# First expert steps: sums of weight blocks on VectorE instead of GpSimd, and most of the gate inside the attention

## The chip, the cores and the metric

The kernel runs on one core of a Trainium2 chip. The metric is the device time of one execution in microseconds (us): before the change the median of 3 runs is 2134.11 us (2133.75 to 2134.13). One further execution was recorded by the profiler and gives all the rows below.

The core has five engines with their own in-order instruction queues: TensorE (PE; its weight loads are shown as PEld), VectorE (DVE), ScalarE (ACT), GpSimd (POOL) and SyncE (SP, which issues the loads here). They run side by side and wait for each other by semaphores.

## The reference

Attention over 4 batches, 8 heads, 1152 keys and 576 queries (each the mean of two neighbours), head dimension 64, and then a mixture of 8 experts on the 2304 tokens that come out:

```python
q_pool = q.reshape(B, H, S // 2, 2, D).mean(axis=3)
scores = scale * np.matmul(q_pool, k.transpose(0, 1, 3, 2))
attn = softmax(scores)                       # with + 1e-09 in the sum
x = matmul(attn, v) as (2304, 512)
logits = x @ w_gate                          # (2304, 8)
P = np.exp(logits - logits.max())
for _ in range(8):                           # Sinkhorn
    P /= P.sum(1, keepdims=True) + 1e-09
    P /= P.sum(0, keepdims=True) + 1e-09
    P *= N / E
for e in range(E):
    out += P[:, e:e+1] * (np.maximum(x @ w1[e], 0.0) @ w2[e])
```

All is float32; w1 is (8, 512, 1024), w2 (8, 1024, 512).

## The kernel before, in words

Two stages follow each other: `attention` and then `moe`.

**Attention.** There are 16 pairs (batch and two heads), each of four full query tiles and one mixed tile. Every operation is entered into a `Plan` with an engine, a cost, a priority (T, in planned microseconds; `PAIR` is the planned length of one pair) and the data and buffers that it reads and writes. `Plan.order` simulates the engines by these costs and writes out one fixed order for all queues; the buffers of a kind ("tr" is a PSUM kind with three buffers, used by transposes and the like) are handed out in order of priority. The result x lies transposed in SBUF: 512 features on partitions in four chunks, 2304 tokens along the free axis. One batch is 576 tokens, or 4.5 token tiles of 128. Near the end the plan also prepares the first token group for the experts (`Blocks`) and loads the first weight blocks and makes their sums on GpSimd (`load_first`, `sums_first`).

**Experts.** `moe` has no order written by hand: the Tile framework's scheduler orders each engine's queue. It first cuts the first w1 block into a high and a low part (`cut1`: L135 on ScalarE, L140 on VectorE), then computes the gate: for all 18 token tiles four matmuls with x as weights and 8 columns of `w_gate` as the moving side, into one PSUM tile `psl` (L630), copied to `PR` by L632. `sinkhorn` is a generator: pieces of its work (small VectorE operations L636 to L658, and an all-reduce over the partitions on GpSimd, L639 once and L654 eight times) are put between the other work by `next(fill)`, four pieces per step.

There are 96 steps: three token groups of 768 tokens, 8 experts, 4 slices of the hidden dimension. A step computes its first product by a Strassen-like scheme of 7 block products (`product`, L671 to L673, each 6 matmuls of 384 columns, since every operand is in two parts). For that, each step's w1 block needs four sums and differences of its quarters: `Weights.sums1`, L121 to L124, four tensor_tensor operations of 128x256 on GpSimd. `sums1(k + 1)` stands in step k behind the third product; `cut1(k + 1)` follows behind the fourth and needs the sums; then the load of the next but one block is issued (one buffer, w1s). VectorE adds up the products out of PSUM (L691) and, with ScalarE, cuts the hidden values (`hidden`, L680 and L681). After every second step, six second products (`second`, L708, 12 matmuls of 512 columns each) are queued, and up to three of them are issued in each of the steps that follow; their results are added to the output, which overwrites x: for the first expert without a weight (L712, L714), later weighted with PR (L717, L718).

Of the kernel before, what the change touches and what calls it, by code (L numbers as in the profile page):

```python
# [5 lines left out]
F32 = mybir.dt.float32  # L6
F32R = mybir.dt.float32r
ACTF = mybir.ActivationFunctionType
# [3 lines left out]
P = 128  # L12
# [4 lines left out]
N, D, E, F = B * Q, H * HD, 8, 1024  # L17
ND = D // P
NT = N // P
# [3 lines left out]
MT = TG // P  # L23
FQ = F // 2 // P
NPAIR = H // 2
NPAIRS = B * NPAIR
# [4 lines left out]
def attention_moe(tc, q, k, v, w_gate, w1, w2, out):  # L31

    nc = tc.nc
    with (  # L40
        tc.tile_pool(name="const", bufs=1) as const,
        tc.tile_pool(name="stage", bufs=1, reuse_waits="tile") as stage,
    ):
        ident = const.tile([P, P], F32, name="ident")
        x = const.tile([P, G, ND, TG], F32, name="x")
        wg = const.tile([P, ND, E], F32, name="wg")

        xch = const.tile([P, 7, 2, TH], F32R, name="xch")
        xcl = const.tile([P, 7, 2, TH], F32R, name="xcl")
        wt = Weights(nc, stage, w1, w2)  # L50
        blocks = Blocks(nc, stage, x, xch, xcl)

        attention(tc, q, k, v, w_gate, x, ident, wg, blocks, wt)
        moe(tc, out, x, xch, xcl, ident, wg, blocks, wt)


class Blocks:
# [32 lines left out]
class Weights:  # L90
# [24 lines left out]
    def sums1(self, k):  # L115

        r = self.raw1[k]
        a11, a12, a21, a22 = r[:, 0, 0:2], r[:, 0, 2:4], r[:, 1, 0:2], r[:, 1, 2:4]
        s = self.sums[k] = self.stage.tile([P, 4, 2, P], F32, name="w1t", tag="w1t")
        e = self.nc.gpsimd  # L120
        e.tensor_tensor(out=s[:, 0], in0=a21, in1=a22, op=ALU.add)  # L121
        e.tensor_tensor(out=s[:, 1], in0=s[:, 0], in1=a11, op=ALU.subtract)
        e.tensor_tensor(out=s[:, 2], in0=a11, in1=a21, op=ALU.subtract)
        e.tensor_tensor(out=s[:, 3], in0=a12, in1=s[:, 1], op=ALU.subtract)  # L124
# [30 lines left out]
class Plan:  # L155
# [18 lines left out]
    def op(self, eng, cost, prio, fn, r=(), w=(), new=(), use=(), lat=0, mode="", after=0):  # L174

        i = len(self.ops)
        deps = set()
        for x in r:
            deps.update(self.writers.get(x, ()))
        for x in w:  # L180
            deps.update(self.writers.get(x, ()))
            deps.update(self.readers.get(x, ()))
        for x in r:
            self.readers.setdefault(x, []).append(i)
        for x in w:
            self.writers[x] = [i]
            self.readers[x] = []
        for name, tag in new:
            self.buf[name] = tag
            self.users[name] = 0  # L190
        mine = [n for n, _ in new] + list(use)
        for n in mine:
            self.users[n] += 1
        deps.discard(i)
        self.ops.append(dict(eng=eng, cost=cost, prio=prio, fn=fn, deps=deps, new=new, mine=mine, lat=lat, mode=mode,
                             after=after, i=i))
# [102 lines left out]
PAIR = QT * UNIT + MIXED  # L299
# [7 lines left out]
    return (n * 2.1 + 150) if two else (n * 3.45 + 100)  # L307


def attention(tc, q, k, v, w_gate, xx, ident, wg, blocks, wt, dry=False, NP=NPAIRS):  # L310


    pairs = [(b, hp) for b in range(B) for hp in range(NPAIR)]
# [7 lines left out]
    D = {}  # L321
    if not dry:
        nc = tc.nc
# [21 lines left out]
    def op(eng, cost, prio, r=(), w=(), new=(), use=(), lat=0, mode="", after=0):  # L345
        def put(fn):
            plan.op(eng, cost, prio, fn, r, w, new, use, lat, mode, after)
        return put

    def pair_ops(p):  # L350
        b, hp = pairs[p]
        first = p == 0
        T = PAIR * (p - 1) if p else -60.0

        @op("SP", 1800, T - 16, w=[("raw", p)], new=[(("kr", p), "kr"), (("qr", p), "qr")], lat=2500)
        def load():
            kr = D["kr", p] = sbt([P, NC, 2, HD], F32, "kr")
            qr = D["qr", p] = sbt([P, 2 * QT + 1, 2, HD], F32, "qr")
            for h in range(2):
                x = q[b, 2 * hp + h]  # L360
                nc.sync.dma_start(out=qr[:, h * QT:(h + 1) * QT],
                                  in_=x[:2 * QM].rearrange("(t p r) d -> p t r d", p=P, r=2))
                nc.sync.dma_start(out=qr[64 * h:64 * h + 64, 2 * QT],
                                  in_=x[2 * QM:].rearrange("(p r) d -> p r d", r=2))
            for h in range(2):
                nc.sync.dma_start(out=kr[:, :, h], in_=k[b, 2 * hp + h].rearrange("(p c) d -> p c d", c=NC))

        @op("SP", 600, T - 6, w=[("v", p)], new=[(("v", p), "vt")], lat=4000)
        def load_v():
            vt = D["v", p] = sbt([P, 2, NC, HD], F32, "vt")  # L370
            nc.sync.dma_start(out=vt, in_=v[b, 2 * hp:2 * hp + 2].rearrange("h (p c) d -> p h c d", c=NC))

        ae = "DVE" if first else "Pool"

        @op(ae, cost(ae, 512, two=True) + 2 * cost(ae, 64, two=True), T + 2, r=[("raw", p)], w=[("qa", p)],
            new=[(("qa", p), "qa")], use=[("qr", p)])
# [12 lines left out]
        for i, (what, c0, n) in enumerate(groups):  # L389
            Ti = T + 6 + 3.4 * i  # L390
            src = [("qa", p)] if what == "q" else [("raw", p)]
            buf = ("qa", p) if what == "q" else ("kr", p)
            tag = what + "T"

# [174 lines left out]


    if NP == NPAIRS:
        T = PAIR * (NP - 5)
        src = [("x", p, mixed) for p in range(2 * NPAIR) for mixed in (False, True)]
        for n, i in enumerate((0, 1, 2, 3, 4, 6, 5)):
            Ti = T + PAIR * n / 3
            if i > 2:
                @op("Pool", 1800, Ti, w=[("T", i)],
                    r=src + {3: [], 4: [("T", 3)], 6: [("T", 4), ("xc", 3, 1)], 5: [("xc", 4, 1), ("T", 6)]}[i])
                def t_add(i=i):
                    blocks.add(0, i, nc.gpsimd)  # L580

            @op("ACT", cost("ACT", 2 * TH), Ti + 2.5, r=src if i < 3 else [("T", i)], w=[("xc", i, 0)])
            def xc_hi(i=i):
                blocks.hi(0, i)

            @op("DVE", cost("DVE", 2 * TH, two=True), Ti + 4, r=[("xc", i, 0)] + [("T", i)] * (i > 2), w=[("xc", i, 1)])
            def xc_lo(i=i):
                blocks.lo(0, i)

        T = PAIR * (NP - 2)  # L590

        @op("SP", 1200, T, w=[("w", 0)], lat=2500)
        def load_first():
            wt.load1(0)
            wt.load2(0)

        @op("Pool", 3000, T + 4, r=[("w", 0)], w=[("w", 1)])
        def sums_first():
            wt.sums1(0)
# [7 lines left out]
        pool.release()  # L607


def moe(tc, out, x, xch, xcl, ident, wg, blocks, wt):  # L610
    nc = tc.nc
    with (
        tc.tile_pool(name="wts", bufs=2, reuse_waits="tile") as wts,
        tc.tile_pool(name="hid", bufs=4, reuse_waits="tile") as hid,
        tc.tile_pool(name="tmp", bufs=1, reuse_waits="tile") as tmp,
        tc.tile_pool(name="gc", bufs=1, reuse_waits="tile") as gc,
        tc.tile_pool(name="gs", bufs=2, reuse_waits="tile") as gs,
        tc.tile_pool(name="ps1", bufs=4, space=PSUM, reuse_waits="tile") as ps1,
        tc.tile_pool(name="ps2", bufs=4, space=PSUM, reuse_waits="tile") as ps2,
# [3 lines left out]
        wt.load1(1)  # L623


        psl = ps2.tile([P, NT, E], F32, name="psl", tag="ps2")
        for m in range(NT):
            g, i = divmod(m, MT)
            for c in range(ND):
                nc.tensor.matmul(psl[:, m, :], x[:, g, c, i * P:(i + 1) * P], wg[:, c, :], start=(c == 0), stop=(c == ND - 1))  # L630
        PR = gc.tile([P, NT, E], F32, name="PR")
        nc.scalar.activation(out=PR, in_=psl, func=ACTF.Copy)  # L632

        def sinkhorn():
            mx = gs.tile([P, 1], F32, name="gmx", tag="gmx")
            nc.vector.tensor_reduce(out=mx, in_=PR, axis=AX.XY, op=ALU.max)  # L636
            yield
# [3 lines left out]
            nc.vector.tensor_scalar(out=nm, in0=mxa, scalar1=-1.0, scalar2=None, op0=ALU.mult)  # L641
            nc.scalar.activation(out=PR, in_=PR, func=ACTF.Exp, bias=nm)
            yield
            for _ in range(8):
                rs = gs.tile([P, NT], F32, name="rs", tag="rs")
                nc.vector.tensor_reduce(out=rs, in_=PR, axis=AX.X, op=ALU.add)
                nc.vector.tensor_scalar(out=rs, in0=rs, scalar1=1e-9, scalar2=None, op0=ALU.add)
                nc.vector.reciprocal(rs, rs)
                nc.vector.tensor_tensor(out=PR, in0=PR, in1=rs.unsqueeze(2).to_broadcast([P, NT, E]), op=ALU.mult)
                cs = gs.tile([P, E], F32, name="cs", tag="cs")  # L650
                nc.vector.tensor_reduce(out=cs, in_=PR.rearrange("p n e -> p e n"), axis=AX.X, op=ALU.add)
                yield
# [77 lines left out]
        for k in range(wt.steps):  # L730
            g, r = divmod(k, FQ * E)
# [60 lines left out]
```

## Time and profile before

| what | value |
|---|---|
| median of 3 runs | 2134.11 us |
| the profiled execution, by its own time | 2129.85 us |
| its span, first to last instruction | 2127.7 us |
| mean granted TensorE clock | 0.984 of full |
| TensorE busy (matmul) | 2073.7 us, 97% |
| VectorE busy | 1468.2 us, 69% |
| ScalarE busy | 900.2 us, 42% |
| GpSimd busy | 363.2 us, 17% |
| attention | 0 to about 538.8 us |
| gate | 538.8 to 565.8 us |
| expert steps | 565.8 us to the end |

Busy times are shares of one execution; an engine that is not the bottleneck may be idle at no cost. Matmuls overlap each other, so that a busy TensorE is not TensorE at its peak, and a matmul's own duration is longer than its distance to the next one. A float32 matmul of the gate appears as two records (144 records of L630 for 72 matmuls). "Issue" in a list of waits is time in which an engine waited for nothing that the profile shows. A granted clock of 1.00 is 2.4 GHz, 0.50 is 1.2 GHz.

### The profile page before, as it was taken

The numbers are of one execution on the slowest core, as the hardware profiler recorded it, in microseconds if no ns is written. First come the engines' busy times: TensorE is split into PE (matmuls) and PEld (weight loads), VectorE is DVE, ScalarE is ACT, GpSimd is POOL, SyncE is SP. The second block draws the span as 40 slices with busy tenths as digits, with TensorE's granted clock in tenths as the row PEclk, the third lists the DMA queues.
The fourth block names the chain that finished last, engine by engine and source line by source line (L and its number), as shares of the span: only waits on it lengthen the run. The fifth ranks groups of instructions, "written<-read, shape, count | busy, mean of one in ns | idle before, by whom it ended". The sixth has DMA issues, their size and how long they took to land.

```text
span 2127.7 us, 34487 instructions
## 1 busy us (share of the span) xinstructions
PE 2073.7 (97%) x13664; PEld 1832.1 (86%) x13664; DVE 1468.2 (69%) x3024; ACT 900.2 (42%) x1594; POOL 363.2 (17%) x456
## 2 busy tenths in 40 slices
PE   9999999999975899999999999999999999999999
PEld 7888888888965899998989999899999999989988
DVE  6666677666344777777776777777778677777774
ACT  5766777666321333333334333333343433333331
POOL 1000101100011322121232211212112221121210
PEclk9999999999788999999999999999999999999999
DMA  5111221200110222221213222222123122222211
GB/s 154 46 57 46 57 68 46 57 24 13 40 60 30 60 78 61 77 62 60 80 55 95 79 70 61 69 70 69 60 79 99 52 78 70 63 67 71 69 60 40
DMA packets 191953, 135.93 MB, mean 64 GB/s; under 512 B 44080, under 2 KB 160816, under 8 KB 191792
## 3 DMA queue, kind: packets, MB, share of 16 engines
q1 hardware_dynamic: 191792, 133.74, 20.9%
q8 instruction: 107, 1.75, 0.3%
q14 instruction: 54, 0.44, 0.1%
HBM read 128.99 MB, written 4.72 MB: 63 GB/s over the span
## 4 chain that ended last, share of the span: by engine, by line
PE 93%; issue 2%; DVE 2%; POOL 1%; DMA 1%; ACT 1%; SPq 0%; POOLq 0%; DVEq 0%; ACTq 0%
PE pso L708 35%; PE psh L671 11%; PE psh L673 11%; PE psh L672 11%; PE tr L488 8%; PE S L448 7%; PE av L516 7%; PE tr L406 1%; PE psl L630 1%; PE tr L545 1%; DVE c L691 0%; DMA w2s<-in_moe_w_dram 0%; DVE hl L681 0%; DVE xcl L87 0%; ACT w1h L135 0%
## 5 line engine op out<-in xcount | busy, mean ns | idle before, releaser
L671 PE MATMUL psh<-xch,w1h 128*128 128x384 f32 x1344 | 457.3, 340 | 44.0 <-ACT w1h L135 41.4
L680 ACT ACTIVATE hh<-c 128x384 fp32r<-128x384 f32 x384 | 200.0, 521 | 674.8 <-DVE c L691 674.8
L673 PE MATMUL psh<-xch,w1l 128*128 128x384 f32 x1344 | 455.2, 340 | 0.0
L672 PE MATMUL psh<-xcl,w1h 128*128 128x384 f32 x1344 | 454.7, 338 | 0.0
L708 PE MATMUL pso<-w2h,hl 128*128 128x512 f32 x1152 | 453.5, 394 | 0.8 <-DVE hl L681 0.8
L708 PE MATMUL pso<-w2l,hh 128*128 128x512 f32 x1152 | 452.9, 393 | 0.0
L708 PE MATMUL pso<-w2h,hh 128*128 128x512 f32 x1152 | 448.0, 389 | 0.0
L718 DVE SCALAR_TENSOR_TENSOR x<-pso,PR,x 128x512 f32<-128x512 f32 x264 | 197.4, 749 | 179.8 <-PE pso L708 179.7
L671 PEld LDWEIGHTS psh<-xch,w1h 128*128 128x128 f32 x1344 | 255.6, 190 | 57.7 <-ACT w1h L135 43.9
L455 DVE TENSOR_SCALAR_CACHE_REDUCE E<-S 128x384 f32<-128x384 f32 x432 | 227.0, 554 | 53.9 <-PE S L448 53.7
L672 PEld LDWEIGHTS psh<-xcl,w1h 128*128 128x128 f32 x1344 | 255.5, 190 | 10.1
L121 POOL TENSOR_TENSOR w1t<-w1s 128x256 f32<-128x256 f32 x96 | 75.2, 784 | 1089.3 <-DMA w1s<-in_moe_w_dram 959.7
L708 PEld LDWEIGHTS pso<-w2h,hl 128*128 128x128 f32 x1152 | 216.0, 188 | 47.0 <-DVE hl L681 1.3
L673 PEld LDWEIGHTS psh<-xch,w1l 128*128 128x128 f32 x1344 | 254.8, 190 | 1.4 <-DVE w1l L140 1.3
L708 PEld LDWEIGHTS pso<-w2l,hh 128*128 128x128 f32 x1152 | 216.1, 188 | 40.2
L708 PEld LDWEIGHTS pso<-w2h,hh 128*128 128x128 f32 x1152 | 216.5, 188 | 39.3 <-ACT hh L680 0.3
L681 DVE SCALAR_TENSOR_TENSOR hl<-c,hh 128x384 fp32r<-128x384 f32 x384 | 240.3, 627 | 13.4 <-ACT hh L680 1.4
L498 ACT ACTIVATE ET<-tr 128x512 f32<-128x512 f32 (+2 forms) x288 | 142.5, 531 | 116.7 <-PE tr L488 116.7
L691 DVE TENSOR_TENSOR c<-psh,u 128x384 f32<-128x384 f32 x288 | 150.9, 553 | 57.3 <-PE psh L673 55.8
L448 PE MATMUL S<-kT,qT 64*128 64x384 f32 (+1 forms) x1296 | 183.2, 365 | 1.7 <-DVE E L455 1.4
L488 PE MATMUL tr<-ident,E 128*128 128x128 f32 x1296 | 182.9, 279 | 0.3 <-DVE ET L500 0.3
L471 ACT ACTIVATE E<-E,st 128x1152 f32<-128x1152 f32 x144 | 179.8, 1253 | 6.0 <-DVE st L461 4.0
(77 smaller groups left out, 2250.9 us busy)
## 6 DMA issues: line engine op xcount, KB each, us to landing
w1s<-in_moe_w_dram SPq DMA_DIRECT2D x192, 256.0 KB, 3.0
w2s<-in_moe_w_dram SPq DMA_DIRECT2D x96, 512.0 KB, 3.5
kr<-in_k_dram SPq DMA_DIRECT2D x32, 288.0 KB, 3.9
vt<-in_v_dram SPq DMA_DIRECT2D x16, 576.0 KB, 3.8
qr<-in_q_dram SPq DMA_DIRECT2D x32, 256.0 KB, 4.1
out_dram<-x SPq DMA_DIRECT2D x18, 256.0 KB, 2.2
qr<-in_q_dram SPq DMA_DIRECT2D x32, 32.0 KB, 3.8
wg<-in_moe_w_gate_dram SPq DMA_DIRECT2D x1, 16.0 KB, 4.8
```

Of the source, the lines that this page charges most:

```text
L448: nc.tensor.matmul(ps[:, h, :PK], D["qT", p][rows, x, t * P:(t + 1) * P], D["kT", p][rows, y, j * PK:(j + 1) * PK], start=(i == 0), stop=( ...
L455: nc.vector.tensor_scalar(out=D["E", m][:, h, j * PK:(j + 1) * PK], in0=D["sc", m, j][:, h, :PK], scalar1=1.0, scalar2=None, op0=ALU.mult, ...
L471: nc.scalar.activation(out=x, in_=x, func=ACTF.Exp, bias=D["st", m][:, h, 3:4], accum_out=D["rs", p][:, t, h:h + 1])
L488: nc.tensor.transpose(ps[:, i * P:(i + 1) * P], x[:, c * P:(c + 1) * P], ident)
L671: nc.tensor.matmul(ps, hi[:, a, c, :], xch[:, b, c, :], start=(c == 0), stop=False)
L672: nc.tensor.matmul(ps, hi[:, a, c, :], xcl[:, b, c, :], start=False, stop=False)
L673: nc.tensor.matmul(ps, lo[:, a, c, :], xch[:, b, c, :], start=False, stop=(c == 1))
L680: nc.scalar.activation(out=hh[:, fh, ts], in_=src, func=ACTF.Relu)
L681: nc.vector.scalar_tensor_tensor(out=hl[:, fh, ts], in0=src, scalar=0.0, in1=hh[:, fh, ts].bitcast(F32), op0=ALU.max, op1=ALU.subtract)
L691: nc.vector.tensor_tensor(out=y, in0=ps, in1=t, op=ALU.add)
L708: nc.tensor.matmul(ps, u[:, fh, ms], w[:, fh, :], start=(n == 0), stop=(n == 11))
L718: nc.vector.scalar_tensor_tensor(out=a, in0=ps, scalar=PR[:, m, e:e + 1], in1=a, op0=ALU.mult, op1=ALU.add)
```

## The change

Two edits. In `Weights.sums1`, the four operations of the blocks 1 to 8 (`2 * FQ` is 8) are issued on VectorE; block 0 and blocks 9 and up stay on GpSimd. And the gate of the token tiles 0 to 12 is computed within the attention's plan: tiles 0 to 8 (tokens of batches 0 and 1) from one pair behind batch 1, tiles 9 to 12 (with batch 2) from one pair behind batch 2, each three planned microseconds behind the one before, each in a "tr" buffer, and copied to PR by VectorE. `moe` computes the last five tiles only. PR moves into the pool of constants.

```diff
+        PR = const.tile([P, NT, E], F32, name="PR")
...
+def gate(nc, ps, x, wg, m):
+
+    g, i = divmod(m, MT)
+    for c in range(ND):
+        nc.tensor.matmul(ps, x[:, g, c, i * P:(i + 1) * P], wg[:, c, :], start=(c == 0), stop=(c == ND - 1))
...
-        e = self.nc.gpsimd
+        e = self.nc.vector if 0 < k <= 2 * FQ else self.nc.gpsimd
...
     if NP == NPAIRS:
+        for bs, lo_m, hi_m in (((0, 1), 0, 9), ((2,), 9, 13)):
+            for m in range(lo_m, hi_m):
+                T = PAIR * (NPAIR * (bs[-1] + 1) + 1) + 3 * (m - lo_m)
+
+                @op("PE", 4 * 115, T, mode="F", r=[("wg",)] + [("x", p, mixed) for p in range(NPAIR * (bs[-1] + 1)) for mixed in (False, True)],
+                    w=[("gt", m)], new=[(("gt", m), "tr")])
+                def gate_mm(m=m):
+                    D["gt", m] = pst([P, 512], "tr")
+                    gate(nc, D["gt", m][:, :E], xx, wg, m)
+
+                @op("DVE", 90, T + 0.5, r=[("gt", m)], w=[("PR", m)], use=[("gt", m)])
+                def gate_out(m=m):
+                    nc.vector.tensor_copy(PR[:, m], D["gt", m][:, :E])
...
-        psl = ps2.tile([P, NT, E], F32, name="psl", tag="ps2")
-        for m in range(NT):
-            g, i = divmod(m, MT)
-            for c in range(ND):
-                nc.tensor.matmul(psl[:, m, :], x[:, g, c, i * P:(i + 1) * P], wg[:, c, :], start=(c == 0), stop=(c == ND - 1))
-        PR = gc.tile([P, NT, E], F32, name="PR")
-        nc.scalar.activation(out=PR, in_=psl, func=ACTF.Copy)
+        M0 = 13
+        psl = ps2.tile([P, NT - M0, E], F32, name="psl", tag="ps2")
+        for m in range(M0, NT):
+            gate(nc, psl[:, m - M0], x, wg, m)
+        nc.scalar.activation(out=PR[:, M0:], in_=psl, func=ACTF.Copy)
```

## Rows read from the trace of the kernel before

**Rows 1.** Page, part 2: busy tenths and granted clock in 40 slices.
```profile
PE   9999999999975899999999999999999999999999
...
PEclk9999999999788999999999999999999999999999
```
**Rows 2.** Windows; columns: window, length, PE, PEld, DVE, ACT, POOL busy, PEclk, DMA.
```profile
300.00:530.00 230.00, 230.00 (x2631) 191.70 (x2628) 156.90 (x531) 162.30 (x304) 15.43 (x16) 1.00 0.14 39
794.00:1100.00 306.00, 306.00 (x1527) 275.96 (x1526) 225.85 (x354) 104.13 (x178) 64.40 (x80) 1.00 0.23 69
```
**Rows 3.** Windows: the gate at either clock, and the expert steps 0 to 7.
```profile
538.77:542.80 4.03, 4.03 (x40) 4.03 (x37) 2.48 (x4) 3.05 (x5) 0.00 (x0) 1.00 0.19 55
542.80:565.80 23.00, 23.00 (x110) 23.00 (x110) 0.00 (x0) 0.00 (x0) 0.00 (x0) 0.50 0.05 15
565.80:730.00 164.20, 120.56 (x555) 107.43 (x556) 96.36 (x207) 46.35 (x77) 30.83 (x41) 0.86 0.17 52
```
**Rows 4.** Waits, 565.8 to 730 us: us in total, times, longest.
```profile
PE psh L671 <- ACT w1h L135: 41.4, 6, 14.5
...
ACT w1h L135 <- POOL w1t L124: 50.1, 8, 17.3
```
**Rows 5.** Timeline of POOL: start us, us, line, operation [idle before <-releaser].
```profile
621.95 0.43 POOL L654 PARTITION_ALL_REDUCE ca<-cs  x1 [5.80 <-issue]
629.41 0.71 POOL L122 TENSOR_TENSOR w1t<-w1t,w1s 128x256 f32<-128x256 f32 x1 [7.03 <-issue]
```
**Rows 6.** Waits of POOL, 565.8 to 730 us.
```profile
POOL w1t L122 <- issue: 30.0, 4, 8.0
...
POOL w1t L121 <- DMA w1s<-in_moe_w_dram: 11.4, 3, 4.0
```
**Rows 7.** Windows: the four stretches of the expert steps at the lower clock.
```profile
565.80:570.10 4.30, 4.30 (x14) 4.30 (x15) 1.44 (x3) 1.60 (x4) 1.15 (x1) 0.50 0.25 62
632.60:638.40 5.80, 5.77 (x17) 5.33 (x18) 3.28 (x5) 1.04 (x2) 0.33 (x1) 0.50 0.30 90
664.00:669.20 5.20, 5.20 (x15) 4.76 (x16) 3.26 (x5) 1.05 (x2) 0.00 (x0) 0.50 0.34 100
694.20:700.00 5.80, 5.76 (x17) 5.32 (x18) 3.37 (x5) 1.04 (x2) 0.43 (x1) 0.51 0.30 90
```
**Rows 8.** Timeline of PE: first and last products of a run at either clock.
```profile
566.27 0.52 PE L672 MATMUL psh<-xcl,w1h 128*128 128x384 f32 x1
...
569.79 0.52 PE L671 MATMUL psh<-xch,w1h 128*128 128x384 f32 x1
...
571.03 0.34 PE L671 MATMUL psh<-xch,w1h 128*128 128x384 f32 x1
...
577.11 0.33 PE L673 MATMUL psh<-xch,w1l 128*128 128x384 f32 x1
```
**Rows 9.** Timeline of DVE around the start of the gate.
```profile
539.15 0.23 DVE L558 TENSOR_TENSOR x<-tr,avs 128x64 f32<-128x64 f32 x1 [1.69 <-ACT avs L535]
...
541.13 1.23 DVE L140 TENSOR_TENSOR w1l<-w1t,w1h 128x1024 fp32r<-128x1024 f32 x1 [0.23 <-ACT w1h L135]
```
**Rows 10.** Timeline of PE at the end of the attention.
```profile
527.79 1.48 PE L516 MATMUL av<-ET,vt 128*64 128x128 f32 x24
...
536.91 0.33 PE L488 MATMUL tr<-ident,E 128*128 128x128 f32 x1 [0.35 <-DVE ET L500]
```
**Rows 11.** Groups by line and shape, 565 to 730 us: busy us, mean ns, idle before.
```profile
L140 DVE TENSOR_TENSOR w1l<-w1t,w1h 128x1024 fp32r<-128x1024 f32 x8 | 9.8, 1224 | 30.3 <-ACT w1h L135 30.3
...
L140 DVE TENSOR_TENSOR w1l<-w1s,w1h 128x256 fp32r<-128x256 f32 x8 | 3.4, 426 | 0.4 <-ACT w1h L135 0.4
...
L123 POOL TENSOR_TENSOR w1t<-w1s 128x256 f32<-128x256 f32 x8 | 7.0, 874 | 0.0
```
**Rows 12.** Windows late in the expert steps 0 to 7.
```profile
711.00:730.00 19.00, 16.30 (x86) 15.11 (x87) 14.99 (x24) 7.11 (x13) 7.31 (x8) 1.00 0.30 84
...
720.00:725.00 5.00, 4.15 (x24) 4.12 (x24) 5.00 (x8) 2.26 (x5) 3.40 (x4) 1.00 0.14 39
```
**Rows 13.** Window with short stops, and the longest stop in it on PE's timeline.
```profile
577.30:602.00 24.70, 20.68 (x100) 17.70 (x98) 15.37 (x35) 10.70 (x17) 6.08 (x8) 1.00 0.27 84
...
602.08 0.44 PE L671 MATMUL psh<-xch,w1h 128*128 128x384 f32 x1 [2.16 <-ACT w1h L135]
```

More of the change, by code (lines that the diff above doesn't have):

```diff
@@ L51, in attention_moe @@
         blocks = Blocks(nc, stage, x, xch, xcl)
-        attention(tc, q, k, v, w_gate, x, ident, wg, blocks, wt)
-        moe(tc, out, x, xch, xcl, ident, wg, blocks, wt)
+        attention(tc, q, k, v, w_gate, x, ident, wg, PR, blocks, wt)
+        moe(tc, out, x, xch, xcl, wg, PR, blocks, wt)
+def gate(nc, ps, x, wg, m):
+    g, i = divmod(m, MT)
+    for c in range(ND):
+        nc.tensor.matmul(ps, x[:, g, c, i * P:(i + 1) * P], wg[:, c, :], start=(c == 0), stop=(c == ND - 1))
 class Blocks:
@@ L307, in cost, with attention @@
     return (n * 2.1 + 150) if two else (n * 3.45 + 100)
-def attention(tc, q, k, v, w_gate, xx, ident, wg, blocks, wt, dry=False, NP=NPAIRS):
+def attention(tc, q, k, v, w_gate, xx, ident, wg, PR, blocks, wt, dry=False, NP=NPAIRS):
     pairs = [(b, hp) for b in range(B) for hp in range(NPAIR)]
@@ L571, in attention @@
     if NP == NPAIRS:
+        for bs, lo_m, hi_m in (((0, 1), 0, 9), ((2,), 9, 13)):
[9 more added lines that the diff above has]
+                    nc.vector.tensor_copy(PR[:, m], D["gt", m][:, :E])
+    if NP == NPAIRS:
         T = PAIR * (NP - 5)
@@ L607, in attention, with moe @@
         pool.release()
-def moe(tc, out, x, xch, xcl, ident, wg, blocks, wt):
+def moe(tc, out, x, xch, xcl, wg, PR, blocks, wt):
     nc = tc.nc
@@ L615, in moe @@
         tc.tile_pool(name="tmp", bufs=1, reuse_waits="tile") as tmp,
-        tc.tile_pool(name="gc", bufs=1, reuse_waits="tile") as gc,
         tc.tile_pool(name="gs", bufs=2, reuse_waits="tile") as gs,
```

## The prediction

> **What bounds the kernel now.** I read the page first. TensorE is busy 97% of the span, but one line of slices breaks the pattern: the granted clock falls in slices 11 to 13 and the busy share in 12 to 14, where the attention ends and the expert stage begins [rows 1]. Everything before and after that hole is TensorE-bound: the attention from 300 to 530 us shows 230.00 us busy of 230, and the settled expert stage 306.00 of 306 [rows 2]. So time can be won only in the hole, and anything added to TensorE outside of it is paid in full.
>
> Then I cut the hole at its events [rows 3]. From 538.8 to 565.8 us TensorE does the gate and nothing else: 4.03 us at a granted clock of 1.00 (2.4 GHz), then 23.00 us at 0.50 (1.2 GHz), on matmuls that are 8 columns wide. From 565.8 to 730 us lie the expert steps 0 to 7: 164.20 us, of which TensorE is busy 120.56, so 43.64 idle. The waits of that stretch name the releaser: the idle time is 41.4 us before L671 for ACT's w1h (L135), and ACT in turn waited 50.1 us for POOL's w1t (L124) [rows 4]. So the sums of weight blocks come late.
>
> Why they do is on POOL's timeline [rows 5]. A sum takes 0.7 us there, and an all-reduce 0.4. But the queue holds them in turns, and each change of kind costs some 7 us in which POOL has nothing to wait for: the all-reduce of 621.95 is done at 622.38, the next sum starts at 629.41 with 7.03 us put down to "issue"; and that all-reduce itself had stood 5.80 us behind the sum before it, put down to "issue" too. The waits grouped show 30.0 us "issue" in 4 cases before L122 alone [rows 6]. There are 9 all-reduces, and the sums of steps 1 to 5 lie between them.
>
> TensorE also pays after long stops: four stretches, 4.30, 5.80, 5.20 and 5.80 us long, run at clock 0.50, the first behind the gate, three behind long stops, the longest 14.5 us [rows 4, 7]. Matmuls of 384 columns are 0.32 us apart there (12 records from 566.27 to 569.79) and 0.174 at clock 1.00 (36 from 571.03 to 577.11) [rows 8].
>
> **The change, part by part.**
>
> *Gate taken out of its own stage.* It is 18 token tiles x 4 matmuls, 144 records (two per matmul). 13 tiles move, 104 records; 40 stay. At clock 1.00 the old gate did 40 records in 4.03 us [rows 3], so the remaining 5 tiles cost 4.03 instead of 27.03: -23.0. The products can follow at once: VectorE has cut the first w1 block at 541.13 + 1.23 = 542.4 us, and the last x that the remaining tiles need is written at 539.15 + 0.23 [rows 9]. If the clock falls at their very end, as it did after 4.03 us, the first 4.3 us of products lose 2.0; I take 0.
>
> *Gate put into the attention.* 104 records at 0.101 us are +10.4, all on the path, since TensorE has no idle time there [rows 2]. Weight loads could hide in part: 24 matmuls of av take 1.48 us, 0.062 each [rows 10], which would make 6.4. Each tile takes one of the three "tr" PSUM buffers until a small copy on VectorE (13 of them; VectorE is busy 157 of 230 us, rows 2, so they cost nothing by themselves; if one came late, a transpose would wait for its buffer). The switch between kinds of matmul is not in the trace as a row of its own; the end of the attention shows one 0.35 us stop for VectorE's eviction of a "tr" buffer [rows 10]. Bounds 0 and 13 x 0.35 = 4.6; I take 1.5, near zero, because the attention switches all the time and shows no idle. Net of the gate: -23.0 + 10.4 + 1.5 = **-11.1 us**. The writes into PR need no new transfer, and wg is loaded in the second pair's time as before.
>
> *Sums of steps 1 to 8 on VectorE.* POOL is left with nothing but all-reduces from step 0 until the sums of step 9, so the changes of kind vanish from the path; the one that stays, back to sums, comes when POOL has long been idle. Removed: the 43.6 us of idle (the 2.2 that are not ACT's are waits for VectorE, which come back in what is late next), and the clock loss: 21.1 us at half clock, of which 1 - 0.174/0.32 = 0.456 is lost, 9.6 us. Together **-53.2 us**.
>
> *What is late next: VectorE.* In 565.8 to 730 us it was busy 96.4 us [rows 3]. It gets 8 x 4 sums of 128x256. The trace has no such sum on VectorE; the nearest row is the subtraction of L140 with the same shape, 0.426 us; by the slope to its larger shape (1.224 - 0.426 us for 768 elements more) the streaming alone is 0.27, and POOL's own 0.874 is the dear end [rows 11]. I take 0.40, a little under the nearest row because records that follow each other overlap: 12.8 us (8.5 to 28.0). VectorE then has 109.2 us to do where TensorE has 164.2 - 43.6 - 9.6 = 111.0. Two engines with the same load and a queue in order cannot both be full. VectorE reached 5.00 of 5 us where it was the one waited for (720 to 725 us), but only 14.99 of 19.00 in 711 to 730 us, where the two waited for each other in turns [rows 12]. At a share of 0.92 it needs 118.7 us, 7.7 more than TensorE; add some 1.3 us until the first product gives it work: **+9 us**. Bounds: 0 (TensorE's work covers VectorE's), and 109.2/0.789 - 111.0 = 27. Behind a sum that waits for its w1s block on VectorE stand the evictions of the products; POOL waited 11.4 us in 3 cases for that load [rows 6]. Steps 0 and 1 are the tight ones, because no second product fills TensorE yet.
>
> Sum: -11.1 - 53.2 + 9 = -55.3. The profiled execution (2129.85 us; span 2127.7) would take 2074.6; the median of the runs stands 4.26 us above it, so 2134.11 - 55.3 = **2078.8 us**.
>
> **The rivals.**
>
> *VectorE becomes the bound in the first steps.* Speaking for it: equal loads, the load of a single w1s buffer now waited for at the head of VectorE's queue, and Sinkhorn's small operations (nine per iteration) in the same queue. Against it: the sums are over in half of POOL's time, which releases the buffer earlier, and Sinkhorn's result is needed first by the second products of steps 4 and 5. With VectorE at 0.75 to 0.79 the rest is 27 to 35 us instead of 9: about 2097 to 2105.
>
> *The change does not do what it says.* Each engine's order in the expert stage is made by the scheduler, not by the program text. If sums and all-reduces still alternated on POOL, only the gate's part would stay: 2134.1 - 11.1 = 2123. Against it: after the diff, POOL has no sum to issue before step 9, and Sinkhorn's 18 pieces, four a step, are spent in step 4.
>
> *Slower: the clock stays at 1.2 GHz through steps 0 to 7.* TensorE's work would be chopped by short waits for VectorE, and 111.0 us at 0.32/0.174 of the pace is 204, 93 us more: about 2163. It decides against the change when over 64.3/0.84 = 77 of the 111 us run at the low level (64.3 is what the other terms without the +9 bring). Against it: the stretches 577.3 to 602 and 711 to 730 us, with 4.0 and 2.7 us of idle in short pieces (the longest of the first 2.16), stayed at 1.00; the low stretches follow the gate and the long stops [rows 7, 12, 13]. The Trainium skill, "TensorE: Matmul & The Clock Gate", section "A second HAM failure mode: psum-queue depth-cycling", tells of a kernel in which frequent micro-idles between groups of matmuls made the clock oscillate; by that rule this rival would have my vote, and this trace disagrees, with clock 1.00 across both stretches with short stops.
>
> **How the numbers follow.** The forecast has 0.74, with a range of its own of 2066 to 2090 (VectorE's rest from 0 with the cheap gate, to 20). VectorE as the bound has 0.17, POOL still alternating 0.03, the low clock 0.03, no change for a reason that I don't see 0.02; the last 0.01 lies below. The range: low 2134.1 - 23.0 + 6.4 - 53.2 = 2064; high with 27 for VectorE and 15.0 for the gate in the attention 2100. A measurement of this kernel can tell about 0.2% (4.3 us) from no change. Faster by more than that 0.95, within 0.02, slower 0.03.
>
> **What would show it.** Right: psl in the expert stage with 40 records in about 4 us at clock 1.00, and 104 records of the gate within the attention at 0.10 us; the attention longer by 10 to 15 us; no "issue" waits before POOL's sums in steps 1 to 8; no stretch of TensorE idle over 5 us and none at 0.50 behind it; the sums on VectorE at about 0.4 us; the rest of the idle time before L671 or L673 now put down to VectorE. Wrong: steps 0 to 7 longer than 138 us; stretches at clock 0.50 in them or in the attention; waits of TensorE for "tr" buffers around the gate tiles; VectorE waiting for w1s at its sums by more than a few us in all.

## The result and the profile after

| what | before | after |
|---|---|---|
| median (4 runs each) | 2133.93 us (2132.02 to 2134.13) | 2070.18 us (2068.61 to 2071.68) |
| ratio after / before | | 0.9703, 95% interval 0.9686 to 0.9720 |
| profiled execution, its span | 2129.85, 2127.7 us | 2071.68, 2069.9 us |

The kernel became 63.75 us faster; 2078.8 us was forecast, with a range of 2064 to 2100. The medians differ by more than the two profiled spans (57.8 us), because the profiled execution of before (2129.85) was faster than all four runs of before, and the one of after the slowest of its four. The accounts below are made on the spans.

The page of the changed kernel, part 2, busy tenths and granted clock, answers to [rows 1]: the hole is gone.

```profile
PE   8999999999999999999999999999999999999999
...
PEclk9999999999999999999999999999999999999999
```

Windows of the changed kernel (columns as in [rows 2]): what is left of the gate at either clock, the first products behind it, and steps 0 to 7, cut so that they hold the same 555 matmul records as the last window of [rows 3]. They answer to [rows 3].

```profile
552.82:554.60 1.78, 1.78 (x20) 1.78 (x16) 0.90 (x3) 1.56 (x4) 0.00 (x0) 1.00 0.00 0
554.60:559.75 5.15, 5.15 (x26) 5.15 (x26) 1.57 (x3) 0.54 (x1) 0.00 (x0) 0.50 0.38 105
559.75:564.10 4.35, 4.35 (x15) 4.35 (x16) 1.58 (x3) 2.46 (x5) 0.38 (x1) 0.50 0.16 29
559.75:672.20 112.45, 112.10 (x555) 101.58 (x556) 102.07 (x246) 49.72 (x84) 7.74 (x13) 0.98 0.25 75
```

Three things are to be seen. The gate's end fell to clock 0.50 after 1.78 us, not after 4.03. The stretch that was 164.20 us long is now 112.45, with 0.35 us of TensorE idle. And VectorE is busy 102.07 us of it, a share of 0.91.

GpSimd's timeline (start us, us, line, operation, idle before and its releaser), first two of the eight all-reduces in the steps, the last, and the first sum after them:

```profile
576.91 0.53 POOL L675 PARTITION_ALL_REDUCE ca<-cs  x1 [15.83 <-DVE cs L672]
583.18 0.63 POOL L675 PARTITION_ALL_REDUCE ca<-cs  x1 [5.75 <-DVE cs L672]
...
624.25 0.40 POOL L675 PARTITION_ALL_REDUCE ca<-cs  x1 [5.87 <-DVE cs L672]
662.67 0.74 POOL L129 TENSOR_TENSOR w1t<-w1s 128x256 f32<-128x256 f32 x1 [38.02 <-DMA w1s<-in_moe_w_dram]
```

Against [rows 5] no "issue" stands before them any more: GpSimd waits for VectorE's data. The all-reduce of 583.18 starts 0.09 us behind the end of the reduction that feeds it (L672, 582.67 + 0.42), so an all-reduce behind an all-reduce pays none of the 6 to 8 us of a change of kind. The one change of kind left falls into a wait of 38 us for a load.

Groups of VectorE's operations in 559.75 to 672.2 us (busy us, mean ns | idle before). The sums' records are 0.394 to 0.417 us long, 13.1 us in all, against 12.8 in the prediction:

```profile
L702 DVE SCALAR_TENSOR_TENSOR hl<-c,hh 128x384 fp32r<-128x384 f32 x32 | 17.2, 547 | 1.2 <-ACT hh L701 0.9
...
L131 DVE TENSOR_TENSOR w1t<-w1s 128x256 f32<-128x256 f32 x8 | 3.3, 417 | 0.0
L129 DVE TENSOR_TENSOR w1t<-w1s 128x256 f32<-128x256 f32 x8 | 3.3, 416 | 0.0
L130 DVE TENSOR_TENSOR w1t<-w1t,w1s 128x256 f32<-128x256 f32 x8 | 3.3, 415 | 0.0
L132 DVE TENSOR_TENSOR w1t<-w1s,w1t 128x256 f32<-128x256 f32 x8 | 3.2, 394 | 0.0
L738 DVE TENSOR_SCALAR x<-x,PR 128x512 f32<-128x512 f32 x6 | 2.9, 491 | 0.0
...
L670 DVE TENSOR_TENSOR PR<-PR,rs 128x144 f32<-128x144 f32 x8 | 2.4, 298 | 0.0
```

TensorE's timeline around one gate tile in the attention (8 records). From its start to the next group are 0.81 us:

```profile
310.83 0.66 PE L496 MATMUL tr<-ident,E 128*128 128x128 f32 x4
311.32 0.96 PE L62 MATMUL tr<-wg,x 128*128 128x8 f32 x8
312.13 0.64 PE L496 MATMUL tr<-ident,E 128*128 128x128 f32 x4
```

The account of the span: the attention 538.77 to 552.82 us (+14.05), the gate's stage 27.03 to 6.93 (-20.1), the expert steps with all that follows 1561.9 to 1510.15 (-51.75). Sum -57.8.

### The profile page after: what moved, and what is told of

Same layout as the page of the kernel before. It is cut to its first block, busy times and chain, and to the rows that moved or that the text cites. A ratio compares the mean times of both kernels' runs of the same rounds, so it can differ in the third digit from the quotient of the medians.

```text
span 2069.9 us, 34422 instructions
## 1 busy us (share of the span) xinstructions
PE 2058.6 (99%) x13664; PEld 1818.8 (88%) x13664; DVE 1463.8 (71%) x3069; ACT 899.7 (43%) x1594; POOL 335.9 (16%) x424
## 4 chain that ended last, share of the span: by engine, by line
PE 95%; DVE 2%; DMA 1%; issue 0%; POOL 0%; ACT 0%; SPq 0%; DVEq 0%; ACTq 0%
PE pso L729 37%; PE psh L692 11%; PE psh L694 11%; PE psh L693 11%; PE tr L496 8%; PE S L456 8%; PE av L524 8%; PE tr L414 1%; PE tr L553 1%; PE tr L62 1%; DMA w1s<-in_moe_w_dram 1%; DVE hl L702 0%; PE psl L62 0%; DVE w1l L148 0%; DVE xcl L95 0%
## 5 line engine op out<-in xcount | busy, mean ns | idle before, releaser
L729 PEld LDWEIGHTS pso<-w2h,hh 128*128 128x128 f32 x1152 | 216.4, 188 | 38.7
L702 DVE SCALAR_TENSOR_TENSOR hl<-c,hh 128x384 fp32r<-128x384 f32 x384 | 229.2, 598 | 13.1 <-ACT hh L701 0.9
```

The lines of the kernel that those rows point to most:

```text
L702: nc.vector.scalar_tensor_tensor(out=hl[:, fh, ts], in0=src, scalar=0.0, in1=hh[:, fh, ts].bitcast(F32), op0=ALU.max, op1=ALU.subtract)
L729: nc.tensor.matmul(ps, u[:, fh, ms], w[:, fh, :], start=(n == 0), stop=(n == 11))
```

## The experiments

The experiments are three sets. The kernels of one set ran on one chip beside the kernel before, whose median there was 2130.8, 2131.05 and 2132.2 us in the three sets. Compare ratios across sets and microseconds within one.

**First set: the two edits apart, and the cause of the stops.**

*Sums alone.* The kernel before with

```diff
-        e = self.nc.gpsimd
+        e = self.nc.vector if 0 < k <= 2 * FQ else self.nc.gpsimd
```

> The sums of blocks 1 to 8 on VectorE, the gate left whole in its own stage as before. Theory A (the two edits are independent, and the expert steps gain the same 51.7 us by which their stretch became shorter in the changed kernel, 1561.9 to 1510.2): about 2082 us (2078 to 2087), TensorE idle in steps 0 to 7 under 3 us, one stretch at clock 0.50 behind the gate. Theory B (VectorE has slack only because the moved gate spares it something): over 2090, with waits of TensorE for VectorE.

Measured: 2078.16 us, ratio 0.9753 (0.9739 to 0.9768), -52.6 us. TensorE's timeline:

```profile
538.71 27.60 PE L630 MATMUL psl<-wg,x 128*128 128x8 f32 x144
566.16 0.67 PE L671 MATMUL psh<-xch,w1h 128*128 128x384 f32 x1
```

The gate is as long as before, and from the first product to the end of the span are 1508.1 us. In steps 0 to 7 the view of waits shows none of TensorE. Theory A holds: VectorE does not need the moved gate for its slack.

*Gate alone.* The changed kernel with `e = self.nc.gpsimd` in `sums1` again.

> The gate of 13 tiles inside the attention, all sums on GpSimd as before. Theory A: the attention is 14.0 us longer and the rest of the gate's stage 20.1 us shorter, so about 2128 us (2123 to 2132), with the stops of 10 us and more in steps 2 to 5 as before. The prediction's own term for the gate (-11.1) would give 2123. Theory B (moving the gate changes where sums and all-reduces meet on GpSimd): outside 2118 to 2134.

Measured: 2120.61 us, ratio 0.9952 (0.9937 to 0.9967), -10.2 us. The stops stayed, as the waits of TensorE from 530 to 760 us show (us in total, times, longest):

```profile
PE psh L692 <- ACT w1h L143: 35.9, 4, 14.0
PE psh L692 <- DVE c L712: 2.8, 2, 2.1
```

They are 38.7 us together instead of 43.6, and the gate's end took 5.24 us here (553.23 to 558.47) instead of 6.93. On the spans, the steps with all that follows became 2.3 us shorter and the gate's end 1.7 us; these make most of the 4 us more than Theory A's -6.1. By ratio (0.9952 of 2133.93 is 2123.7) the result lies within A's bounds, near their lower end. The two edits add up: -52.6 - 10.2 = -62.8, 2.95% of 2130.8, where both together brought 2.97%, and 2.85% in the second set.

*Copies in place of the all-reduces.*

```diff
-                nc.gpsimd.partition_all_reduce(ca, cs, channels=P, reduce_op=bass.bass_isa.ReduceOp.add)
+                nc.gpsimd.tensor_copy(ca, cs)
...
-            nc.gpsimd.partition_all_reduce(mxa, mx, channels=P, reduce_op=bass.bass_isa.ReduceOp.max)
+            nc.gpsimd.tensor_copy(mxa, mx)
```

> The kernel before, with the nine all-reduces replaced by plain copies of the same small tiles on GpSimd (the sum and the maximum over the partitions are left out). Queue, waits and the sums' place on GpSimd stay, only the kind of the small operation changes. Theory A (the stops come from the change of kind on GpSimd, some 7 us each way): the waits put down to issue vanish and TensorE's idle time in steps 0 to 7 falls from 43.6 us to under 8; about 2087 us (2080 to 2095). Theory B (GpSimd is simply too slow for the sums, 3.1 us a block against 1.6): most of the idle time stays, over 2115 us.

Measured: 2084.78 us, ratio 0.9782 (0.9766 to 0.9799), -46.0 us, with all sums still on GpSimd. Waits of TensorE behind the gate, the copies' group on GpSimd, and one group of VectorE:

```profile
PE psh L671 <- DVE c L691: 2.0, 3, 1.0
PE pso L708 <- DVE w2l L151: 1.0, 1, 1.0
PE psh L671 <- DVE u L691: 0.6, 1, 0.6
```

```profile
L654 POOL COPY ca<-cs 128x8 f32<-128x8 f32 x8 | 2.6, 321 | 22.4 <-DVE cs L651 22.4
```

```profile
L649 DVE TENSOR_TENSOR PR<-PR,rs 128x144 f32<-128x144 f32 x8 | 3.5, 433 | 0.0
```

Theory A holds: it is the change of kind on GpSimd that made the stops; a copy that stands in the same queue with the same waits does not. What is left to the speed of the sums themselves is 6.6 us (2084.78 against 2078.16 with the sums on VectorE), of which TensorE's waits behind the gate are 4.3 us, the three above and two shorter ones. They are VectorE's in the main, and the last row shows a reason why VectorE is later here: the same operation took 433 ns in the mean where GpSimd's additions run beside some of its eight, and 298 in the changed kernel, where GpSimd has none to do.

*One chunk of the gate tiles in the attention.*

```diff
-                    gate(nc, D["gt", m][:, :E], xx, wg, m)
+                    g, i = divmod(m, MT)
+                    nc.tensor.matmul(D["gt", m][:, :E], xx[:, g, 0, i * P:(i + 1) * P], wg[:, 0, :], start=True, stop=True)
```

> The changed kernel with only one of the four chunks of each of the 13 gate tiles inside the attention (26 records in place of 104; three quarters of these tiles' logits are left out). Their places in the plan, buffers and copies stay. Theory A (a record costs 0.10 us, the remaining 3.6 of the 14.0 us belong to the places: buffers, switches, changed order): 78 records less, 7.8 us: about 2062.4 us (2060.5 to 2064.5), the attention 546 us long. Theory B (the records cost all of it, 0.135 us each): 2059.7 us or less. Theory C (the places cost most): over 2066.

Measured: 2062.7 us, ratio 0.9680 (0.9665 to 0.9694). That is 5 to 7.5 us below the changed kernel by the ratios of its two measurements (0.9703 and 0.9715). The attention is 545.77 us long, as Theory A had it:

```profile
545.77 5.25 PE L62 MATMUL psl<-wg,x 128*128 128x8 f32 x40
```

A finer measure are the distances between the pairs (the 16 records that spread the row sums, L545 before and L553 in the changed kernel, once per pair): 33.02 us from pair to pair without gate tiles. In the changed kernel four intervals are longer, 34.34, 40.68, 34.35 and 35.81, together 13.1 us more; here they add up to 5.4. That makes 0.099 us a record and some 0.2 us a place. The remaining 1 us of the attention's 14.05 lies before any gate tile: the first pair's records start at 42.36 us before, at 43.7 after and between 42.3 and 44.4 in the other profiles.

**Second set: where the clock fell, the places, and VectorE's room.**

*The changed kernel again.*

> The changed kernel once more, as the reference on this chip for the three runs beside it. About 0.970 of the kernel before. Its gate stage was 6.9 us long in the first profile, with the clock falling 1.8 us into it, and 5.2 to 5.4 us in two related kernels: if the fall comes at another moment each time, this stage lies again between 4.0 and 7.

Measured: 2071.17 us (2068.54 to 2071.74), ratio 0.9715 (0.9702 to 0.9728). Its gate's end lasted from 553.52 to 559.27, 5.75 us, within the 4.0 to 7 expected.

*The last gate tiles spread.*

```diff
-        for m in range(M0, NT):
+        M1 = 15
+        for m in range(M0, M1):
             gate(nc, psl[:, m - M0], x, wg, m)
...
+            if k == 0:
+                nc.vector.scalar_tensor_tensor(out=wg2, in0=c11[:, :ND * E].rearrange("p (c e) -> p c e", c=ND), scalar=0.0,
+                                               in1=wg, op0=ALU.mult, op1=ALU.add)
             u2 = plus(product(k, 4, 4), p1, "u2")
+            rest()
```

`rest` does one of the tiles 15 to 17 with wg2; it stands twice more, behind u3 and c22, and Sinkhorn begins behind it.

> The changed kernel with the last three gate tiles held back behind the first products of step 0 (they read a copy of w_gate that a small VectorE operation makes after the second product), so that only 16 records cover the wait for the first cut. Theory A (8-column matmuls in one run let the clock fall, and the low clock behind them costs 1 to 3 us in the gate and 2 in the first products): no stretch at 0.50 around the start of step 0, 2 to 5 us less than the changed kernel. Theory B (the first cut is late, and the pause for it takes what the clock gives back): within 1.5 us of it, with TensorE idle for 2 us or more at the start of step 0.

Measured: 2066.49 us (2066.33 to 2067.49), ratio 0.9699 (0.9686 to 0.9712), 4.7 us less than the changed kernel beside it. Timeline and windows of TensorE:

```profile
553.23 1.95 PE L62 MATMUL psl<-wg,x 128*128 128x8 f32 x16
555.04 0.43 PE L701 MATMUL psh<-xch,w1h 128*128 128x384 f32 x1
```

```profile
553.20:563.00 9.80, 9.80 (x75) 9.77 (x71) 7.35 (x15) 4.90 (x9) 0.00 (x0) 1.00 0.38 109
563.00:573.00 10.00, 10.00 (x57) 9.78 (x58) 9.31 (x25) 5.51 (x12) 0.91 (x2) 1.00 0.18 52
```

Theory A: the clock stays at 1.00, and the first product follows without a pause. This version beats both kernels. It does not keep the clock up in every variant: see the first kernel of the third set.

*Two gate tiles in one place of the attention.* The plan's loop steps by two tiles, with one "tr" buffer, one copy and twice the cost in the plan:

```diff
-            for m in range(lo_m, hi_m):
+            for m0 in range(lo_m, hi_m, 2):
...
-                    gate(nc, D["gt", m][:, :E], xx, wg, m)
+                    for i, m in enumerate(ms):
+                        gate(nc, ps[:, i * E:(i + 1) * E], xx, wg, m)
```

> The changed kernel with the 13 gate tiles inside the attention taken two at a time (7 places, buffers and copies in place of 13; the same 104 records). Theory A (by the run with one chunk a record costs 0.09 us and each place about 0.36): six places less, about 2 us shorter, attention 550.5 us instead of 552.8. Theory B (what was left over is the changed order as a whole, not a price for each place): the attention stays at 552 to 553.5. Theory C (16 records in a row let the clock fall): a window under 1.00 in the attention and no gain.

Measured: 2072.14 us, ratio 0.9723 (0.9710 to 0.9736), no gain. The attention ends at 556.05, and its four longer intervals (36.77, 39.97, 36.80, 36.11) are together 17.6 us longer than without gate tiles, for the same 104 records; that is 4.5 more than with single tiles. Three of the six places with two tiles, and the windows behind them:

```profile
304.03 1.95 PE L62 MATMUL tr<-wg,x 128*128 128x8 f32 x16
...
446.82 1.95 PE L62 MATMUL tr<-wg,x 128*128 128x8 f32 x16
...
459.68 1.85 PE L62 MATMUL tr<-wg,x 128*128 128x8 f32 x16
...
556.05 6.34 PE L62 MATMUL psl<-wg,x 128*128 128x8 f32 x40
```

```profile
306.10:308.88 2.78, 2.78 (x22) 2.01 (x21) 0.58 (x4) 1.39 (x2) 0.00 (x0) 0.50 0.00 0
449.46:452.24 2.78, 2.78 (x24) 2.29 (x22) 1.04 (x4) 0.00 (x0) 0.00 (x0) 0.50 0.00 0
463.11:465.89 2.78, 2.78 (x15) 2.45 (x16) 1.01 (x6) 1.67 (x4) 0.00 (x0) 0.50 0.00 0
```

Theory C: behind three of the six groups of 16 records the clock fell to 0.50, for 2.78 us each time; behind the groups of 8 in the attention it fell in no profile. If such a stretch loses the 0.456 that the prediction worked out, the three cost 3.8 of the 4.5 us (an estimate). Theory A's gain of 2 us does not appear even with these taken off, since 13.8 remain against 13.1 with single tiles.

*Sums computed twice.*

```diff
+        for _ in range(2 if 0 < k <= 2 * FQ else 1):
-        e.tensor_tensor(out=s[:, 0], in0=a21, in1=a22, op=ALU.add)
+            e.tensor_tensor(out=s[:, 0], in0=a21, in1=a22, op=ALU.add)
...
```

> The changed kernel with the sums of blocks 1 to 8 computed twice on VectorE (13 us more work for it in steps 0 to 7, the same result). The prediction's view (VectorE and TensorE have equal loads there and each us more on VectorE is waited for): 9 to 13 us more, TensorE idle in steps 0 to 7 for that long. Theory B (VectorE's load was lower than I worked out, 104 us against 113, and its order leaves room): less than 5 us more.

Measured: 2073.71 us (2072.45 to 2074.69), ratio 0.9732 (0.9718 to 0.9745), 2.5 us more than the changed kernel beside it. Waits of TensorE, 530 to 760 us, and windows of the first 80 us:

```profile
PE pso L730 <- DVE w2l L160: 0.9, 1, 0.9
PE psh L693 <- ACT p L708: 0.9, 2, 0.6
```

```profile
560.00:600.00 40.00, 38.42 (x192) 34.26 (x191) 36.37 (x99) 17.83 (x32) 2.73 (x4) 0.97 0.21 66
600.00:640.00 40.00, 39.78 (x198) 35.18 (x197) 38.69 (x108) 16.21 (x27) 1.79 (x4) 1.00 0.22 67
```

13 us more on VectorE cost 2.5: Theory B. VectorE is busy 38.69 of the 40 us from 600 to 640, and TensorE still does 39.78. The changed kernel had as much there already; first its window, then the one of the doubled sums that holds the same 555 matmul records as [rows 3]:

```profile
600.00:640.00 40.00, 39.65 (x196) 35.14 (x195) 38.84 (x99) 17.03 (x29) 2.02 (x4) 1.00 0.27 80
```

```profile
558.53:673.00 114.47, 112.67 (x555) 100.30 (x556) 107.61 (x271) 47.03 (x79) 5.01 (x10) 0.98 0.23 70
```

In that stretch VectorE's busy time rose by 5.5 us (102.07 to 107.61), not by 13: records overlap, and some of VectorE's work was done after the stretch (271 operations, where 32 more than the 246 would be 278). The load that the prediction worked out was 109.2, not 113.

**Third set: variants of the spread gate.**

*The plan's cost of a gate tile.* `4 * 115` becomes `4 * 200`.

> The kernel with the spread gate (last three tiles behind the first products), and in the attention's plan a gate tile entered at 4*200 ns instead of 4*115, near the 0.81 to 1.06 us that it takes. Theory A (part of the 13.1 us that the attention grows by is disorder from the wrong cost in the plan, beyond 10.4 for the records): the intervals between pairs grow by 10.5 to 11.5 us in sum instead of 13.1, total 0.9690 to 0.9698 of before where the spread gate alone had 0.9699. Theory B (the plan's cost of a gate tile does not matter): within 1 us of it, the intervals grow by 12.5 to 13.7.

Measured: 2067.56 us, ratio 0.9696 (0.9683 to 0.9709); the four intervals (34.34, 40.38, 34.35, 35.91) are 12.9 us longer. Theory B: this cost does not matter. In this profile the clock did fall once, behind two groups of gate records in step 0 that the scheduler had drawn close together (16 from 558.33 us, 8 from 560.46):

```profile
562.25:565.25 3.00, 3.00 (x11) 3.00 (x10) 2.50 (x5) 1.71 (x3) 0.00 (x0) 0.50 0.58 174
```

*All sums but the first on VectorE.* `0 < k <= 2 * FQ` becomes `k`.

> The kernel with the spread gate, and the sums of all blocks but the first on VectorE, in all 96 steps. Theory A (GpSimd's additions slow VectorE's two-operand operations beside them, and nothing more: TensorE is the bound in the settled steps): the mean of the hl operation (scalar_tensor_tensor, 128x384) in 800 to 1100 us falls from 0.64 us to 0.55, the total within 2 us of the spread gate's, 0.9699 of before. Theory B (VectorE becomes the bound with 1.6 us more a step): slower by 10 us or more.

Measured: 2066.94 us, ratio 0.9696 (0.9683 to 0.9709), the same. The hl operation in 800 to 1100 us, first in the spread gate's kernel, then here:

```profile
L711 DVE SCALAR_TENSOR_TENSOR hl<-c,hh 128x384 fp32r<-128x384 f32 x77 | 48.5, 630 | 4.0 <-ACT hh L710 1.3
```

```profile
L711 DVE SCALAR_TENSOR_TENSOR hl<-c,hh 128x384 fp32r<-128x384 f32 x77 | 44.0, 572 | 2.7 <-ACT hh L710 0.3
```

Theory A in the time, and in its direction for hl: without GpSimd's additions VectorE is quicker by 58 ns an operation, less than the 90 expected.

*No gate in the attention.* The plan's gate operations go; two tiles stand before the first product, sixteen in four groups of four between the products of step 0.

> The kernel with the spread gate, and no gate in the attention at all: two tiles cover the wait for the first cut, sixteen stand in four groups of four between the products of step 0. Theory A (a record costs 0.10 us at full clock wherever it stands, and the attention's disorder goes): the attention back at 538.8 us, 10.4 us more in step 0, so 2 to 3 us less in all than the spread gate, about 0.9687 of before. Theory B (groups of 32 eight-column records let the clock fall): a stretch at 0.50 in step 0, and no gain or a loss of up to 5 us.

Measured: 2076.49 us, ratio 0.9739 (0.9726 to 0.9753), 9.5 us more than the kernel with all sums on VectorE beside it, and 0.4% more than the spread gate by ratio. The attention is back at 538.5 us and all its full intervals are 33.05 us at most, but the timeline and the windows show:

```profile
538.53 1.95 PE L62 MATMUL psl<-wg,x 128*128 128x8 f32 x16
545.32 10.58 PE L62 MATMUL psl<-wg,x 128*128 128x8 f32 x64
```

```profile
545.30:549.00 3.70, 3.70 (x34) 3.70 (x33) 2.69 (x7) 2.00 (x2) 0.00 (x0) 0.96 0.22 83
549.70:576.00 26.30, 26.30 (x115) 26.30 (x115) 3.95 (x7) 0.81 (x2) 0.38 (x1) 0.50 0.05 15
```

Theory B, and by more than it had: the scheduler drew two groups of four together, the clock fell and stayed at 0.50 for 26.3 us, in which TensorE was never idle.

## Why the prediction was right, and where it was off

*The cause of the stops: right, and shown.* The idle time (43.6) and the low clock behind the stops went, and neither came back as another wait. The copies show that it was the change of kind, the sums alone that the second edit was not needed for it.

*VectorE late next, +9 us: the term that was mis-sized; it measured about 0.* From the first product on the span shortened by 51.75 us. Of the 53.2 forecast, 2.0 stayed with the gate (its first products still ran at 0.50), so what VectorE cost is 53.2 - 2.0 - 51.75, or 0 within about half a microsecond. Two steps of the working failed. VectorE's load was not 96.4 + 12.8 = 109.2 but 102.07. In part its own operations became shorter without GpSimd's additions beside them (hl from 605 ns in the same view of before to 547, L717's scaling from 559 to 491); in part a record starts before the one ahead of it ends (the first two sums at 566.15 and 566.48, 0.42 us long each), so that 32 sums add less busy time than their lengths. At the prediction's own share of 0.92 a load of 102.07 takes 111 us, no more than TensorE's 111.0: the load alone takes the term away. And from nearly equal loads it does not follow that TensorE waits: from 600 to 640 us both were busy for over 38.8 of 40 us, and twice the sums cost 2.5. I take the second products for the reason, work that needs nothing new from VectorE; that alone was not tested. The rival in which VectorE becomes the bound had the same error larger.

*Gate out of its stage, -23.0: measured -20.1,* and the 2.0 above were lost besides. I took the clock to hold for the 4.03 us that it held before. It fell after 1.78 us in the profile of after; the stage lasted 5.1 to 6.9 us in the six profiles that have its 40 records in one run. The loss that I set to 0 was 4.9 us, and the spread gate gave 4.7 back.

*Gate into the attention, +11.9: measured 13.1* by the intervals between pairs, with 0.099 us a record, as assumed. The +1.5 for switches is some 2.7. What they consist of stays open: two tiles per place did not lower them, but in that kernel the clock fell, which hides a price per place of a few tenths of a microsecond.

*The sum.* -23.0 + 11.9 - 53.2 + 9 became -20.1 + 14.05 - 51.75: the forecast was 8 us too careful in one term, and 5 us too bold in the two of the gate. That the sum came out within 3 us (-57.8 on the spans for -55.3) owes something to luck, since these errors cancel. The median beat the forecast by 8.6 us, and most of that is no step of the mechanism: the prediction put the median 4.26 us above the profiled execution, as before the change, and after it the median lies 1.5 below.

*The signs.* Of the signs named for being wrong one showed, a stretch at clock 0.50 in step 0, 4.35 us long. Of those named for being right two failed: the gate's 40 records did not stay at 1.00, and hardly any idle time before the products was left to put down to VectorE (0.35 us in all).

*The low clock (rival): not seen.* With short stops in steps 0 to 7 (1.8 us in all in the run with doubled sums, 4.3 in the one with copies), the clock was at 1.00 there except for the stretch that follows the gate. The rule of the Trainium skill that was weighed for it ("TensorE: Matmul & The Clock Gate", section "A second HAM failure mode: psum-queue depth-cycling") has no support in any run here.

## What to carry to other kernels

Look for an engine that has nothing to wait for and still stands still: two kinds of work in turns on GpSimd cost 6 to 8 us at each turn here, and taking one kind off was worth 46 of the 52.6 us, the faster sums only the rest. Before you fear the engine that receives the work, ask which work of the bound engine needs it, and count that its own operations may become shorter. Put narrow matmuls one small group at a time between dense ones (in the attention here the clock held behind groups of 8 records, and fell behind three of six groups of 16); in a run of their own they lower TensorE's clock for what follows too.

## What the runs showed of the hardware that I had not expected

- A TensorE that is busy without a pause still fell to 1.2 GHz on 8-column matmuls, and 1.78 us into them in the profile of the changed kernel, 4.03 in that of the kernel before. In the kernel with two tiles in one place it also fell behind three of the six groups of 16 records that stand between other matmuls.
- VectorE's operations lengthen beside GpSimd's additions: a 128x144 tensor_tensor from 298 to 433 ns, the 128x384 scalar_tensor_tensor from 547 to 605 in the first steps and from 572 to 630 in the settled ones. These are means of operations with and without an addition beside them. Taken one by one, in the kernel before from 800 to 860 us, twelve of sixteen hl operations took 0.55 or 0.56 us and the four that overlap additions 0.90 to 1.01. One of either, and GpSimd's records around the second:

```profile
806.84 0.55 DVE L681 SCALAR_TENSOR_TENSOR hl<-c,hh 128x384 fp32r<-128x384 f32 x1
...
811.68 1.01 DVE L681 SCALAR_TENSOR_TENSOR hl<-c,hh 128x384 fp32r<-128x384 f32 x1
```

```profile
811.53 0.75 POOL L121 TENSOR_TENSOR w1t<-w1s 128x256 f32<-128x256 f32 x1 [12.09 <-DMA w1s<-in_moe_w_dram]
812.23 1.05 POOL L123 TENSOR_TENSOR w1t<-w1s 128x256 f32<-128x256 f32 x1
```

- The first pair of the attention reached its row sums at 42.3 to 44.4 us in the profiles of kernels that do the same up to there: up to 2 us of a span are decided before the change has a part in it.
